# A linear attention and a SiLU MLP on one core: five column blocks in the first load of W1, three in its next, and smaller edits at the start of the kernel

## The chip, the cores and the metric

The kernel runs on one core of a Trainium2 chip. The metric is the time of one execution on the device, in microseconds. The kernel before was run three times; the median is what the changed kernel is compared with. A core has five engines that run their own instruction streams: TensorE (PE, matmuls; PEld is its weight loads), VectorE (DVE), ScalarE (ACT), GpSimd (POOL) and SyncE (SP). They meet at semaphores. Transfers between HBM and the core's SBUF are issued by an engine's queue and run on 16 DMA engines; here SP and ScalarE issue through one kind of queue, GpSimd through another.

## What is computed

The inputs are q, k and v of 8 batches, 8 heads, 576 positions and 64 columns, and two weight matrices, W1 (512 x 2048) and W2 (2048 x 512), all float32. The attention is a linear one: q goes through a softmax over its 64 columns, k through a softmax over the positions, and

```python
kv = np.einsum('bhsd,bhse->bhde', k_s, v)
x = np.einsum('bhsd,bhde->bhse', q_s, kv)     # then heads side by side: 4608 x 512
h = x @ w_in
g = h * (1.0 / (1.0 + np.exp(-h)))
out = g @ w_out                                # 4608 x 512, float32
```

Nearly all the arithmetic is in the two products with W1 and W2.

## The kernel before

The rows of x are worked on in nine chunks (t = 0 to 8) of 512. Chunk 0 is done plainly, with W1 and W2 as they are; its first layer takes all 576 positions of batch 0, so that chunk 1 has only 448 left. The chunks after it use a scheme of seven products per block (`group`, `prod`) that replaces eight by seven and needs sums and differences of blocks of the weights (`ws_op`, `t_op`) and of the data (`xs_op`, `s_op`), which VectorE makes.

The work's order is a list written out by hand, `ORDER`: a string of names, each bound to a small function, called in turn. What one engine does follows that list in its order; across engines only the data's dependences count. So a name that moves in the list past names of other engines keeps its place on its own engine.

The names around the change:

- `lq0.0`, `lk0.0`, `lv0.1.0` and so on load halves of q, k and v of a batch (line 151); those of batch 0 are issued by SP, those of batches 1 and 2 by GpSimd, later ones by SP again.
- `gate` (line 627) is a tiny copy on GpSimd that reads the first half of k of batch 0, so that GpSimd's weight loads start after that has landed.
- `W1a0`, `W1a1`, `W1b`, `W1c`, `W1d` load W1 (line 566). They are issued by GpSimd because they cast from float32 to float16 on the way. W1 has 16 column blocks of 128 columns and 4 row chunks c of 128 rows. Before, W1a0 brings blocks 0 to 3 of chunks 0 and 1, W1a1 the same blocks of chunks 2 and 3, and W1b, W1c and W1d bring four blocks each, all chunks. `W2a` to `W2d` load W2 (line 572) behind them.
- The first layer of chunk 0: `w{fb}.0` and `w{fb}.1` (`wide_mm`, line 306) are the matmuls of column block fb with chunks 0 and 1, then 2 and 3, four each; `h{fb}` (line 319) is the tanh on ScalarE; `v{fb}` (line 322) combines it on VectorE. Each block has a pair of PSUM banks given by `WIDE`; the next block in that pair must wait for the `v` of the one before. `p{fb}` (line 444) is the second layer of chunk 0.
- `vc0.1a`, `vc0.1b`, `vc0.1c` cast the last half of v of batch 0 to bf16 (lines 142 and 144): c takes one pair of heads on GpSimd, a and b share the other pair between ScalarE and VectorE by position blocks j (nine of them). `kv0.1.0` and `kv0.1.1` (line 247) are the matmuls on them; `kc0.1` divides by the sums; `X0.1` (line 281) makes the second half of x of chunk 0; `x0.0a`, `x0.1a` (ScalarE) and `x0.0v`, `x0.1v` (VectorE) copy x out of PSUM.
- In batch 2: `lq2.1` loads the second half of q, `eq2.1` (line 162) is its exp on ScalarE, `z2.1` (lines 206 and 210) its sums and reciprocals on VectorE. In chunk 1, `s1...` (line 142 or 144) copies a pair of PSUM banks to SBUF, `a1...` (line 402) adds another pair to it, and the next `g1...` (line 424) into these banks waits for that. `p15` stands among them in the list.
- `touch` reads a few scattered elements of k, v and W1 at the very start, 64 each, ahead of the large loads; nothing reads what it brings.

Of the kernel before, what the change touches and what calls it, by code (L numbers as in the profile page):

```python
# [16 lines left out]

ORDER = """
    lq0.0 lq0.1 lk0.0 lv0.0 lk0.1 lv0.1.0 lv0.1.1 gate W1a0 W1a1 W1b W1c heat0 eq0.0.0 z0.0.0 eq0.0.1 z0.0.1 eq0.1
    n0.0 ek0.0 z0.1 tr0.0 vc0.0 heat1 n0.1 tc0.0b kv0.0 tc0.0a kc0.0 tr0.1 ek0.1 vc0.1b X0.0 tc0.1b  # L20
    vc0.1a vc0.1c W1d lq1.0 lq1.1 W2a kv0.1.0 kv0.1.1 kc0.1 tc0.1a x0.0v X0.1 x0.0a x0.1v w0.0 w2.0 w1.0 x0.1a W2b1 lk1.0 w1.1 h1 w0.1 w3.0 w2.1
    W2b2 w3.1 h0 v1 v0 w5.0 w5.1 w4.0 w4.1 h2 v2 h3 w6.0 w6.1 h5 v3 h4 v5 w7.0 w7.1 h7 WS1.1 w9.0 v4 h6 w9.1 WS0.1
    w8.0 w8.1 v7 lk1.1 h9 h8 w11.0 v6 eq1.0.0 w11.1 v9 v8 h11 WS1.2 w10.0 lv1.1 w10.1 v11 w12.0 w12.1 eq1.0.1 W2c1
    h10 w13.0 lv1.0 v10 w13.1 w15.0 h12 h13 qp1a w15.1 v12 qp1b h15 v13 w14.0 eq1.1.0 z1.0 w14.1 eq1.1.1 p0 WS0.3 p1
    v15 z1.1.0 WS1.4 W2c2 z1.1.1 h14 lq2.0 n1.0 p2 ek1.1 n1.1 p3 v14 p4 vc1.1b tr1.0 ek1.0 tc1.0a p5 p6 W2d vc1.1a
    p7 p8 gcopy tr1.1 WS1.3 lq2.1 vc1.0 p9 T1 tc1.1a tc1.0b tc1.1b kv1 WS0.2 p10 kc1 xt1.0 xt1.1 lk2.0 eq2.0 x1.1v
    p11 x1.0a g1.1.1 x1.3v x1.2a s1.1.0a xs1.1 xs1.2 g1.1.2 p12 z2.0 eq2.1 g1.1.6 xs1.3 lk2.1 xs1.4 s1.1.1a p13 z2.1
    lv2.0 p14 lv2.1 ek2.0 n2.0 ek2.1 n2.1 vc2.0 a1.1.0 g1.1.7 p15 s1.1.2v tq2 po2v g1.1.5 a1.1.2 g1.1.4 po1a po3v
    lk3.0 vc2.1 po0a m3 u1.1.4 mu3 T3 g1.1.3 m2 lq3.0 u1.1.2 m1 u1.1.0 lq3.1 a1.1.1 m0 mu1 mu0 lk3.1 mu2 lv3.0
    u1.1.1 T2 kv2 kc2 m5 mu5 T4 m4 mu4 m7 X2.0 lv3.1 WS0.4 vc3.1 mu7 X2.1 x2.1a x2.0v m6 x2.2v os0 x2.3a vc3.0 mu6  # L30
    g2.1.1 ek3.0 b1.2.0 b1.1.0 xs2.1 xs2.2 s2.1.0v S1.1 g2.1.6 g2.1.2 S1.2 xs2.3 xs2.4 b1.1.1 eq3.1 b1.2.1 s2.1.1a
    a2.1.0 g2.1.7 ek3.1 g2.1.5 lk4.0 eq3.0 z3.1 g2.0.2 s2.1.2a g2.1.4 sa1 a2.1.2 g2.1.3 n3.1 u2.1.4 b1.6.1 os1 z3.0
    a2.1.1 g2.0.1 u2.1.0 b1.6.0 n3.0 lq4.0 u2.1.2 wa1 s2.0.0a b1.5.0 lk4.1 S1.3 kv3 u2.1.1 S1.4 sb1 g2.0.6 tq3
# [30 lines left out]
    wb7 S8.1b e1.1 o7.0 S8.1a b7.4.1 S8.2a sa8 S8.2b e2.0 wl7v e6.0 S8.3 o7.1 e6.1 e2.1 sb8 e5.0 waE0 S8.4 qa00g
    qa01s e7.0 waE1 e7.1 qa11g qa10a e5.1 sc8 wcE0 e3.0 wcE1 qc01g wxE0 qc11a e3.1 wbE0 qc00a wxE1 qb00g qb01s e4.0
    wbE1 qc10s qb10g e4.1 qb11s wlE0a ql01a ql00s wlE1a ql11a ql10s
"""


# [1 line left out]
def kernel(  # L71
# [9 lines left out]
    nc = tc.nc  # L81
# [4 lines left out]
    J = S // P  # L86
# [45 lines left out]
    T3 = B12  # L132
# [165 lines left out]
        o0 = pieces(t)[0][3]  # L298
        copy(eng, XTS[t % 2][:, c, o0:TCH], PS[:, XBANK[c], o0:TCH])

    WIDE = (4, 2, 0, 6) * 4

    def wide_mm(fb, cs):
        for n in range(2):
            for c in cs:
                nc.tensor.matmul(  # L306
                    out=PS[:, WIDE[fb] + n, 0:S // 2],
                    lhsT=W1[:, c, fb * 128:(fb + 1) * 128],
# [241 lines left out]
    def touch(i, x, eng):  # L550
        rows4 = x.rearrange("(a p z) f -> p a z f", a=4, p=16)
        eng.dma_start(out=touched[:, i, :, None], in_=rows4[:, :, 0, 0:1])
# [144 lines left out]
    for t in range(1, NCH):  # L697
# [6 lines left out]
        for g in range(2):  # L704
            n = f"{t}.{g}."
# [123 lines left out]
```

## Time and profile before

| what | value |
|---|---|
| median of 3 runs | 256.89 us (256.43 to 257.05) |
| the profiled execution's own time | 257.51 us |
| its span, first to last instruction | 255.7 us |
| granted TensorE clock, mean | 0.999 of full speed |
| read from HBM, written to it | 36.70 MB, 9.44 MB |

The time of an execution has 1.8 us that lie outside the span. A row of a timeline gives the start and the length in us, the engine and line, the operation, the tensors written and read with their shape, the number of instructions merged into the row, and in brackets how long the engine was idle before and what ended that. Matmuls overlap each other, so the busy time of a row is longer than the time from its start to the next row's start. A row of DMA issues gives the tensor, the queue, the number, the size of one and the median time from issue to landing. What releases an instruction is inferred from semaphores, so a chain can name a neighbour of the true cause.

### The profile page before, as it was taken

How to read it: one execution, taken by the hardware profiler on the slowest of the kernel's cores; microseconds unless marked ns; L12 is line 12 of the kernel's file. 1: busy time of each engine (PE TensorE's matmuls, PEld its weight loads, DVE VectorE, ACT ScalarE, POOL GpSimd, SP SyncE). 2: the span in 40 equal slices, each digit the busy share in tenths (PEclk: the TensorE clock that was granted, in tenths of full speed). 3: DMA queues.
4: the chain of work that ended last, by engine and by line, in shares of the span. 5: the costliest groups of instructions: out<-in, count | busy, mean ns of one | idle time of the engine just before them, and what ended most of it. 6: DMA issues, size and time to landing. Idle time of an engine off the chain costs nothing.

```text
span 255.7 us, 6428 instructions
## 1 busy us (share of the span) xinstructions
PE 247.9 (97%) x2712; PEld 204.3 (80%) x2712; DVE 205.7 (80%) x277; ACT 190.6 (75%) x226; POOL 66.7 (26%) x64
## 2 busy tenths in 40 slices
PE   7789999999999999999999999999999999999994
PEld 3367755666888888888888888888888888888883
DVE  3868998899999998998987986896569836886752
ACT  4765867899999999999879979737587666664411
POOL 2563872540360631530083040006000000000022
PEclk9999999999999999999999999999999999999999
DMA  7999999879959947996964950021807000700365
GB/s 231 350 200 298 270 337 328 310 150 382 388 117 242 404 158 181 349 307 165 301 246 87 243 198 3 3 61 24 170 6 160 6 0 4 154 11 3 69 139 124
DMA packets 36205, 45.90 MB, mean 180 GB/s; under 512 B 16448, under 2 KB 21248, under 8 KB 36176
## 3 DMA queue, kind: packets, MB, share of 16 engines
q1 hardware_dynamic: 29424, 33.56, 45.1%
q0 software_dynamic: 6192, 11.60, 17.6%
q10 hardware_dynamic: 560, 0.33, 0.6%
q8 instruction: 21, 0.34, 0.6%
q14 instruction: 8, 0.07, 0.1%
HBM read 36.70 MB, written 9.44 MB: 180 GB/s over the span
## 4 chain that ended last, share of the span: by engine, by line
PE 89%; DMA 7%; DVE 1%; POOL 1%; ACT 1%; SPq 0%; issue 0%; ACTq 0%
PE PS L502 37%; PE PS L424 35%; PE PS L444 5%; PE PS L306 5%; DMA W<-in_moe_w_in_dram 4%; DMA kt<-in_k_dram 3%; PE PS L334 2%; PE PS L247 2%; PE PS L281 2%; DMA out_dram<-ow 1%; POOL W L566 1%; DVE h L144 0%; PE PS L233 0%; SPq L151 0%; DVE ow L763 0%; ACT ow L776 0%
## 5 line engine op out<-in xcount | busy, mean ns | idle before, releaser
L402 DVE TENSOR_TENSOR h<-PS,h 128x1024 f32<-128x1024 f32 (+1 forms) x45 | 54.1, 1205 | 9.5 <-PE PS L424 7.8
L502 PEld LDWEIGHTS <-GT 128*128 128x128 f16 x512 | 50.0, 98 | 6.0
L424 PEld LDWEIGHTS <-WS 128*128 128x128 f16 x480 | 46.6, 98 | 6.8 <-issue 1.0
L408 ACT ACTIVATE GT<-h 128x1024 f16<-128x1024 f32 (+1 forms) x45 | 46.7, 1050 | 0.9 <-DVE h L402 0.8
L502 PE MATMUL PS<-W,GT 128*128 128x256 f16 x384 | 47.2, 273 | 0.0
L424 PE MATMUL PS<-XS,WS 128*128 128x256 f16 (+1 forms) x360 | 45.0, 272 | 0.0
L142 ACT COPY h<-PS 128x1024 f32<-128x1024 f32 (+1 forms) x31 | 31.1, 1003 | 16.9 <-PE PS L424 15.8
L502 PEld LDWEIGHTS <-S 128*128 128x128 f16 x384 | 37.1, 98 | 4.7
L424 PEld LDWEIGHTS <-W 128*128 128x128 f16 x360 | 35.1, 98 | 4.5 <-issue 0.2
L215 POOL TENSOR_TENSOR eq<-eq,rzq 128x1152 bf16<-128x1152 bf16 x13 | 27.7, 2139 | 36.0 <-DVE rzq L210 35.8
L144 POOL CAST vaug<-vt 128x1152 bf16<-128x1152 f32 (+1 forms) x13 | 16.3, 1268 | 61.4 <-DMA vt<-in_v_dram 53.3
L502 PE MATMUL PS<-T,S 128*128 128x256 f16 x256 | 32.0, 273 | 0.0
L424 PE MATMUL PS<-XT,W 128*128 128x256 f16 (+1 forms) x240 | 29.9, 272 | 0.0
L144 DVE COPY h<-PS 128x1024 f32<-128x1024 f32 (+1 forms) x14 | 17.0, 1212 | 8.6 <-PE PS L424 3.7
L162 ACT ACTIVATE eq<-qt 128x1152 bf16<-128x1152 f32 (+1 forms) x19 | 18.8, 1008 | 4.6 <-DMA qt<-in_q_dram 4.6
L781 POOL DMA_DIRECT2D out_dram<-ow x5 | 2.7, 545 | 70.0 <-DVE ow L763 70.0
L167 ACT ACTIVATE ek<-kt 128x1152 bf16<-128x1152 f32 x16 | 18.4, 1161 | 3.3 <-DMA kt<-in_k_dram 3.2
L408 ACT ACTIVATE GT<-PS 128x1024 f16<-128x1024 f32 (+1 forms) x15 | 15.2, 1014 | 6.6 <-PE PS L424 6.5
L206 DVE TENSOR_REDUCE zq<-eq 128x18 f32<-128x1152 bf16 x13 | 17.5, 1346 | 1.2 <-ACT eq L162 0.9
L306 PE MATMUL PS<-XT,W 128*128 128x288 f16 x128 | 16.0, 286 | 0.4 <-DMA W<-in_moe_w_in_dram 0.4
L502 PE MATMUL PS<-T,GT 128*128 128x256 f16 x128 | 16.3, 273 | 0.0
L502 PE MATMUL PS<-W,S 128*128 128x256 f16 x128 | 16.1, 273 | 0.0
(86 smaller groups left out, 332.8 us busy)
## 6 DMA issues: line engine op xcount, KB each, us to landing
out_dram<-ow SPq DMA_DIRECT2D x64, 128.0 KB, 3.3
qt<-in_q_dram SPq DMA_DIRECT2D x12, 576.0 KB, 5.7
kt<-in_k_dram SPq DMA_DIRECT2D x12, 576.0 KB, 7.1
vt<-in_v_dram SPq DMA_DIRECT2D x11, 576.0 KB, 6.9
qt<-in_q_dram POOLq DMA_DIRECT2D x4, 576.0 KB, 11.9
kt<-in_k_dram POOLq DMA_DIRECT2D x4, 576.0 KB, 12.6
vt<-in_v_dram POOLq DMA_DIRECT2D x4, 576.0 KB, 12.1
W<-in_moe_w_in_dram POOLq DMA_DIRECT2D x3, 512.0 KB, 10.4
```

The source lines that it names most:

```text
L142: eng.copy(out=o, in_=i)
L144: eng.tensor_copy(o, i)
L162: nc.scalar.activation(out=half(st[b]["eq"], cc)[:, :, g0:g1], in_=jgd(b, "qt", cc)[:, :, g0:g1], func=ACT.Exp)
L167: nc.scalar.activation(out=half(ek, cc), in_=jgd(b, "kt", cc), func=ACT.Exp)
L206: nc.vector.reduce_sum(out=z, in_=e, axis=AX.X)
L215: eng.tensor_tensor(out=e, in0=e, in1=r[:, :, :, None].to_broadcast([128, J, 2, D]), op=ALU.mult)
L306: nc.tensor.matmul(out=PS[:, WIDE[fb] + n, 0:S // 2], lhsT=W1[:, c, fb * 128:(fb + 1) * 128], rhs=XTS[0][:, c, n * (S // 2):(n + 1) * (S / ...
L402: nc.vector.tensor_tensor(out=four(t, i), in0=group_bank(t, g), in1=four(t, i), op=ALU.add)
L408: nc.scalar.activation(out=group_out(t, f, n), in_=x, func=ACT.Silu, scale=1.0 / XS)
L424: nc.tensor.matmul(out=PS[:, bank + p // 2, (p % 2) * HT:(p % 2) * HT + width(t)], lhsT=a[:, c, p * 128:(p + 1) * 128], rhs=bb[:, c, 0:wid ...
L444: nc.tensor.matmul(out=PS[:, 2 + tb, :], lhsT=GTS[t % 2][:, fc, tb * 128:(tb + 1) * 128], rhs=W2[:, fc, :], start=(fc == 0), stop=(fc == N ...
L502: nc.tensor.matmul(out=PS[:, bank, m * HN:(m + 1) * HN], lhsT=a[:, fc, m * 128:(m + 1) * 128], rhs=bb[:, fc, :], start=(first and fc == 0) ...
```

## The change

Five things are edited. The two loads W1a0 and W1a1 bring five column blocks each instead of four, and W1b three instead of four. Blocks 4 and 5 trade places: block 4 now comes ahead of block 5 in the list, with its matmuls, tanh and combination, and their PSUM banks trade places with them. In the list `x0.1a` comes ahead of `x0.1v` and of block 0's matmuls. Of the nine position blocks of v's last cast ScalarE takes four and VectorE five; before it was five and four. The small read of W1 is issued on ScalarE's queue, behind those of k and v, and no longer on GpSimd's.

```diff
-    vc0.1a vc0.1c W1d lq1.0 lq1.1 W2a kv0.1.0 kv0.1.1 kc0.1 tc0.1a x0.0v X0.1 x0.0a x0.1v w0.0 w2.0 w1.0 x0.1a W2b1 lk1.0 w1.1 h1 w0.1 w3.0 w2.1
-    W2b2 w3.1 h0 v1 v0 w5.0 w5.1 w4.0 w4.1 h2 v2 h3 w6.0 w6.1 h5 v3 h4 v5 w7.0 w7.1 h7 WS1.1 w9.0 v4 h6 w9.1 WS0.1
+    W1d lq1.0 lq1.1 W2a kv0.1.0 kv0.1.1 kc0.1 tc0.1a x0.0v X0.1 x0.0a x0.1a x0.1v w0.0 w2.0 w1.0 W2b1 lk1.0 w1.1 h1
+    w0.1 w3.0 w2.1 W2b2 w3.1 h0 v1 v0 w4.0 w4.1 w5.0 w5.1 h2 v2 h3 w6.0 w6.1 h4 v3 h5 v4 w7.0 w7.1 h7 WS1.1 w9.0 v5
...
-    WIDE = (4, 2, 0, 6) * 4
+    WIDE = (4, 2, 0, 6, 2, 4, 0, 6) + (4, 2, 0, 6) * 2
...
-    touch(2, w_in, nc.gpsimd)
+    touch(2, w_in, nc.scalar)
...
-    for x, eng, g, j0, j1 in (("a", nc.scalar, 1, 0, 5), ("b", nc.vector, 1, 5, J), ("c", nc.gpsimd, 0, 0, J)):
+    for x, eng, g, j0, j1 in (("a", nc.scalar, 1, 0, 4), ("b", nc.vector, 1, 4, J), ("c", nc.gpsimd, 0, 0, J)):
...
-    for x, f, n, c0, c1 in (("W1a0", 0, 4, 0, 2), ("W1a1", 0, 4, 2, 4), ("W1b", 4, 4, 0, 4), ("W1c", 8, 4, 0, 4), ("W1d", 12, 4, 0, 4)):
+    for x, f, n, c0, c1 in (("W1a0", 0, 5, 0, 2), ("W1a1", 0, 5, 2, 4), ("W1b", 5, 3, 0, 4), ("W1c", 8, 4, 0, 4), ("W1d", 12, 4, 0, 4)):
```

The rest of the list holds the same names in the same order; its lines are only broken elsewhere.

More of the change, by code (lines that the diff above doesn't have):

```diff
@@ L24 @@
[L24 to L33, printed above, removed]
@@ L64 @@
[L64 to L66 removed]
+    n0.0 ek0.0 z0.1 tr0.0 vc0.0 heat1 n0.1 tc0.0b kv0.0 tc0.0a kc0.0 tr0.1 ek0.1 vc0.1b X0.0 tc0.1b vc0.1a vc0.1c
+    W1d lq1.0 lq1.1 W2a kv0.1.0 kv0.1.1 kc0.1 tc0.1a x0.0v X0.1 x0.0a x0.1a x0.1v w0.0 w2.0 w1.0 W2b1 lk1.0 w1.1 h1
@@ new lines @@
+    w0.1 w3.0 w2.1 W2b2 w3.1 h0 v1 v0 w4.0 w4.1 w5.0 w5.1 h2 v2 h3 w6.0 w6.1 h4 v3 h5 v4 w7.0 w7.1 h7 WS1.1 w9.0 v5
+    h6 w9.1 WS0.1 w8.0 w8.1 v7 lk1.1 h9 h8 w11.0 v6 eq1.0.0 w11.1 v9 v8 h11 WS1.2 w10.0 lv1.1 w10.1 v11 w12.0 w12.1
+    eq1.0.1 W2c1 h10 w13.0 lv1.0 v10 w13.1 w15.0 h12 h13 qp1a w15.1 v12 qp1b h15 v13 w14.0 eq1.1.0 z1.0 w14.1
+    eq1.1.1 p0 WS0.3 p1 v15 z1.1.0 WS1.4 W2c2 z1.1.1 h14 lq2.0 n1.0 p2 ek1.1 n1.1 p3 v14 p4 vc1.1b tr1.0 ek1.0
+    tc1.0a p5 p6 W2d vc1.1a p7 p8 gcopy tr1.1 WS1.3 lq2.1 vc1.0 p9 T1 tc1.1a tc1.0b tc1.1b kv1 WS0.2 p10 kc1 xt1.0
@@ new lines @@
+    xt1.1 lk2.0 eq2.0 x1.1v p11 x1.0a g1.1.1 x1.3v x1.2a s1.1.0a xs1.1 xs1.2 g1.1.2 p12 z2.0 eq2.1 g1.1.6 xs1.3
+    lk2.1 xs1.4 s1.1.1a p13 z2.1 lv2.0 p14 lv2.1 ek2.0 n2.0 ek2.1 n2.1 vc2.0 a1.1.0 g1.1.7 p15 s1.1.2v tq2 po2v
+    g1.1.5 a1.1.2 g1.1.4 po1a po3v lk3.0 vc2.1 po0a m3 u1.1.4 mu3 T3 g1.1.3 m2 lq3.0 u1.1.2 m1 u1.1.0 lq3.1 a1.1.1
+    m0 mu1 mu0 lk3.1 mu2 lv3.0 u1.1.1 T2 kv2 kc2 m5 mu5 T4 m4 mu4 m7 X2.0 lv3.1 WS0.4 vc3.1 mu7 X2.1 x2.1a x2.0v m6
+    x2.2v os0 x2.3a vc3.0 mu6 g2.1.1 ek3.0 b1.2.0 b1.1.0 xs2.1 xs2.2 s2.1.0v S1.1 g2.1.6 g2.1.2 S1.2 xs2.3 xs2.4
@@ new lines @@
+    u4.0.1 xs5.1 g5.1.1 xs5.2 wb3 b3.4.1 s5.1.0v o2.1 ek7.1 g5.1.2 kc6 g5.1.6 wl3a xs5.3 xs5.4 a5.1.0 lv7.0 b4.2.0
+    s5.1.1a lv7.1 b4.1.0 S4.1 eq7.1 g5.1.7 ek7.0 b4.2.1 s5.1.2v o3.1 g5.1.5 S4.2 b4.1.1 u5.1.0 a5.1.2 g5.1.4 sa4
+    g5.0.2 o3.0 u5.1.4 wa4 g5.1.3 S4.3 u5.1.2 vc7.1 g5.0.1 b4.6.0 a5.1.1 vc7.0 s5.0.0a b4.6.1 a5.0.0 u5.1.1 g5.0.6
+    S4.4 b4.5.0 s5.0.1a b4.5.1 sb4 u5.0.0 g5.0.7 g5.0.5 s5.0.2v b4.7.0 eq7.0 a5.0.2 b4.7.1 z7.1 g5.0.4 sc4 g5.0.3
+    b4.4.0 a5.0.1 u5.0.4 b4.4.1 wc4 u5.0.1 X6.0 X6.1 kv7 x6.0v u5.0.2 x6.3v b4.3.0 x6.1a kc7 b4.3.1 x6.2a xs6.1
@@ new lines @@
+    S7.3 g8.1.3 u8.1.4 g8.0.2 a8.1.1 u8.1.2 g8.0.1 u8.1.1 b7.6.0 s8.0.0v b7.6.1 wa7 g8.0.6 a8.0.0 sb7 b7.5.0 s8.0.1a
+    S7.4 b7.7.0 g8.0.7 g8.0.5 s8.0.2v b7.7.1 a8.0.2 b7.5.1 sc7 u8.0.0 g8.0.4 wc7 g8.0.3 u8.0.4 b7.4.0 a8.0.1 u8.0.2
+    b7.3.0 u8.0.1 b7.3.1 e1.0 wb7 S8.1b e1.1 o7.0 S8.1a b7.4.1 S8.2a sa8 S8.2b e2.0 wl7v e6.0 S8.3 o7.1 e6.1 e2.1
+    sb8 e5.0 waE0 S8.4 qa00g qa01s e7.0 waE1 e7.1 qa11g qa10a e5.1 sc8 wcE0 e3.0 wcE1 qc01g wxE0 qc11a e3.1 wbE0
+    qc00a wxE1 qb00g qb01s e4.0 wbE1 qc10s qb10g e4.1 qb11s wlE0a ql01a ql00s wlE1a ql11a ql10s
```

57 lines of the change are left out of this document (25 added, 32 removed).

## The prediction

> **What bounds the kernel now.** I read the head of the page first, then the chain that ended last in order of time, then the timelines of TensorE, ScalarE and VectorE where the chain names something other than TensorE, and last the loads.
>
> ```profile
> span 255.7 us, 6428 instructions
> PE 247.9 (97%) x2712; PEld 204.3 (80%) x2712; DVE 205.7 (80%) x277; ACT 190.6 (75%) x226; POOL 66.7 (26%) x64
> ```
>
> TensorE is busy for 97% of the span, so a gain must start its stream earlier or close a hole in it, and then survive to the end. The chain names one load ahead of the long stretches of matmuls, and the timeline of PE (start, length, line, count, idle time before) shows what it costs:
>
> ```profile
> 10.04 9.22 DMA W<-in_moe_w_in_dram
> ...
> 50.43 1.09 DVE h L144
> ```
>
> ```profile
> 14.81 4.09 PE L306 MATMUL PS<-XT,W 128*128 128x288 f16 x32
> 19.31 11.93 PE L306 MATMUL PS<-XT,W 128*128 128x288 f16 x96 [0.40 <-DMA W<-in_moe_w_in_dram]
> 31.08 4.48 PE L444 MATMUL PS<-W,GT 128*128 128x512 f16 x20
> ```
>
> Line 306 is the first layer of batch 0: sixteen column blocks of eight matmuls. Blocks 0 to 3 run from 14.81; then W1b, issued at 10.04, lands 9.22 later at 19.26, and blocks 5, 4, 6 and so on run without a hole until line 444 starts at 31.08. From start to start that is 11.77 us for 96, or 0.1226 us each. The 32 before would have been done feeding at 14.81 + 32 x 0.1226 = 18.73, so the hole is 0.58 us in starts (0.40 between busy times).
>
> Does a gain there reach the end? The chain's DVE piece at 50.43 made me look at 45 to 52, first PE, then what feeds VectorE (ACT, DVE rows), then the load behind that (POOL's issue, and its time to landing):
>
> ```profile
> 45.43 1.03 PE L444 MATMUL PS<-W,GT 128*128 128x512 f16 x4
> 46.29 0.93 PE L424 MATMUL PS<-XS,WS 128*128 128x224 f16 x8
> 47.06 1.89 PE L444 MATMUL PS<-W,GT 128*128 128x512 f16 x8
> ...
> 49.55 1.03 PE L444 MATMUL PS<-W,GT 128*128 128x512 f16 x4
> 50.57 0.93 PE L424 MATMUL PS<-XS,WS 128*128 128x224 f16 x8
> 51.56 0.93 PE L424 MATMUL PS<-XS,W 128*128 128x224 f16 x8
> ```
>
> ```profile
> 46.72 1.16 ACT L162 ACTIVATE eq<-qt 128x1152 bf16<-128x1152 f32 x1 [0.96 <-DMA qt<-in_q_dram]
> ```
>
> ```profile
> 47.92 1.35 DVE L206 TENSOR_REDUCE zq<-eq 128x18 f32<-128x1152 bf16 x1 [0.89 <-ACT eq L162]
> 49.31 0.27 DVE L210 RECIPROCAL rzq<-zq 128x18 f32<-128x18 f32 x1
> 49.49 1.03 DVE L402 TENSOR_TENSOR h<-PS,h 128x896 f32<-128x896 f32 x1
> 50.43 1.08 DVE L144 COPY h<-PS 128x896 f32<-128x896 f32 x1
> ```
>
> ```profile
> 34.67 0.73 POOL L151 DMA_DIRECT2D qt<-in_q_dram  x1
> ```
>
> ```profile
> qt<-in_q_dram POOLq DMA_DIRECT2D x1, 576.0 KB, 12.0
> ```
>
> Four matmuls of line 444 take 0.86 from start to start (45.43 to 46.29), eight of line 424 take 0.77 (46.29 to 47.06). The p15 of 49.55 is thus fed by 50.41, but the next group starts at 50.57, just after VectorE's addition (a1.1.0) ends at 50.52 and frees its banks: a wait of 0.16. That group is fed by 51.34, yet the following one starts at 51.56, after the copy (s1.1.2v) ends at 51.51: another 0.22. The busy rows overlap and hide both. VectorE is dense from 47.92, where it had idled 0.89 for eq2.1; that had idled 0.96 on ScalarE for the load lq2.1, which lands at 34.67 + 12.0 = 46.7. **So around 51 us the kernel hangs on a load, and TensorE arrives there 0.38 us too early already.** The loads before it are back to back: the share of the DMA engines (next to last column) never falls below one.
>
> ```profile
> core 0: us, PE busy (x) PEld busy (x) DVE busy (x) ACT busy (x) POOL busy (x), PEclk, DMA share, GB/s
> ...
> 12.00:24.00 12.00, 10.74 (x127) 7.93 (x125) 7.99 (x15) 7.29 (x13) 6.47 (x9) 1.00 1.20 231
> 24.00:36.00 12.00, 12.00 (x90) 8.20 (x88) 11.38 (x18) 8.76 (x16) 9.32 (x10) 1.00 1.14 307
> 36.00:47.00 11.00, 11.00 (x147) 6.44 (x144) 9.72 (x19) 8.19 (x12) 3.20 (x5) 1.00 1.11 333
> ```
>
> **The change part by part.**
>
> *Five and three blocks.* The 0.58 us hole sits ahead of the fifth block because that block is in W1b. With five blocks in W1a0 and W1a1, each of them is 320 KB instead of 256, and W1b 384 instead of 512; the megabyte of the three is the same, so I take W1b's landing as it is, 19.26.
>
> ```profile
> 8.55 3.00 POOL L566 DMA_DIRECT2D W<-in_moe_w_in_dram  x4
> ```
>
> ```profile
> W<-in_moe_w_in_dram POOLq DMA_DIRECT2D x1, 256.0 KB, 6.0
> ...
> W<-in_moe_w_in_dram POOLq DMA_DIRECT2D x1, 256.0 KB, 6.5
> ...
> DMA packets 1208, 1.21 MB, mean 202 GB/s; under 512 B 41, under 2 KB 1207, under 8 KB 1207
> ```
>
> The four issues take 0.75 each, so W1a0 (8.55) lands at 14.5 and W1a1 (9.3) at 15.8. Between 13 and 19 us the queue writes 202 GB/s, so 64 KB more take 0.32: W1a0 at 14.84, W1a1 (two times 64 KB behind) at 16.48. Both now come late: the first block could start at 14.76 (next edit) and starts at about 14.89; block 1's second half (w1.1, the thirteenth matmul) could start at 14.89 + 12 x 0.1226 = 16.36 and waits until 16.53. From there 116 matmuls without a hole end their feeding at 16.53 + 14.22 = 30.75, against 31.08: **0.33 us gained at the start of line 444**, not 0.58. Block 5 is due at 16.53 + 28 x 0.1226 = 19.96, with 0.7 to spare to W1b. The issues on POOL that wait for these landings go out up to 0.65 later, into a queue that lands things 12 us after their issue: no cost while the backlog stands.
>
> By the fit of the Trainium skill (page "DMA: Bandwidth & Descriptors", section "Anatomy of one DMA — SWDGE (gpsimd) path": 2.0 us plus bytes over 436 GB/s), 64 KB more would be an estimated 0.15, W1a1 would land at 16.13 and delay nothing, and the gain would be 0.63; the trace's 202 GB/s for these casting loads disagrees with that rate.
>
> *Blocks 4 and 5 swapped* in the list and in their banks, and x0.1a moved up: the banks come round in the order they had, ScalarE's own order is unchanged but for the two swapped tanh. Cost 0.
>
> *VectorE's five ninths of the last v cast.*
>
> ```profile
> 12.86 0.47 ACT L142 CAST vaug<-vt 128x320 bf16<-128x320 f32 x1 [0.15 <-DMA vt<-in_v_dram]
> 12.86 0.29 DVE L144 CAST vaug<-vt 128x256 bf16<-128x256 f32 x1 [0.71 <-DMA vt<-in_v_dram]
> ...
> 37.61 0.67 ACT L142 CAST vaug<-vt 128x576 bf16<-128x576 f32 x1
> ...
> 37.42 0.75 DVE L144 CAST vaug<-vt 128x576 bf16<-128x576 f32 x1
> ```
>
> By the 576-column rows, 64 columns are 0.05 on ScalarE and up to 0.12 on VectorE. ScalarE's part ends at 13.28 instead of 13.33, VectorE's at 13.24 to 13.27 instead of 13.15: the later of both gains 0.05, which the matmuls of line 247, X0.1 and block 0 inherit (14.81 to 14.76). VectorE's qT copy behind it slips by the same 0.1, and only X0.1, just ahead of 14.81, needs it. W1a0's landing then eats the gain.
>
> *The small read of W1 on ScalarE's queue.*
>
> ```profile
> kvn<-in_k_dram ACTq DMA_DIRECT2D x1, 0.2 KB, 3.2
> kvn<-in_moe_w_in_dram POOLq DMA_DIRECT2D x1, 0.2 KB, 5.0
> kvn<-in_v_dram ACTq DMA_DIRECT2D x1, 0.2 KB, 4.2
> ...
> out_dram<-ow POOLq DMA_DIRECT2D x5, 64.0 KB, 2.1
> ...
> vt<-in_v_dram SPq DMA_DIRECT2D x2, 288.0 KB, 8.4
> ```
>
> ```profile
> 1.33 0.67 POOL L552 DMA_DIRECT2D kvn<-in_moe_w_in_dram  x1 [0.89 <-POOLq L813]
> 1.34 0.43 ACTq L552 DMA_DIRECT2D kvn<-in_v_dram  x1
> ...
> 3.56 1.35 SPq L151 DMA_DIRECT2D vt<-in_v_dram  x2
> ```
>
> (The last column of the first five rows is us to landing.) POOL loses an issue of 0.67; the next issue there that anything waits for is W1a0's at 8.55. ScalarE's queue gets a third issue of some 0.43 ahead of the first exp, which waits for q anyway. It is one more on the two hardware queues: SP's last two issues took 1.35 for two because the second waited for an earlier load's landing; now the one before it may wait as well, up to 1 us. Both land 8.4 us after their issue, behind loads that keep the engines full: 0. The open price is whether POOL's first real load, W1a0, then pays for being the first of its queue. Below: 0, as all loads run on the same engines. Above: the small read took 5.0 on POOL, against 4.2 for v's on ScalarE (1.33 and 1.34, at the same time) and 2.1 for POOL's stores at the end, so between 0.8 and 2.9. I take 0, since the 4.2 shows that most of the 5.0 is the crowd of that moment. The Trainium skill says the same on that page, section "Issuing engines are not separate DMA queues": the issuing engine saves only issue time.
>
> **The sum.** Start of line 444: -0.33. At 50.57 and 51.56: TensorE, already 0.38 early, becomes 0.7 early; lq2.1 lands when it did, since the bytes ahead of it are the same. After 51.56 nothing moves. Span 255.7, change 0 (with -0.05 for small things). The profiled execution took 257.51, 0.62 over the median of 256.89; against the median I predict **256.8**.
>
> **The rivals.** 0.3% is 0.77 us, about what a measurement of this kernel can tell from no change.
>
> *A, likeliest, no change:* as summed, 256.5 to 257.2. For it: the idle times before eq2.1 and z2.1. Against: the profiled execution is slower than the median, perhaps just in its loads.
>
> *B, faster:* lq2.1 does not decide, because the loads run sooner (W1's first megabyte is 5.2 us of the queue, now in rows of 2560 and 1536 bytes instead of 2048; 10% on it would be 0.5). TensorE's gain then passes, 0.33, or 0.63 if W1a1 is in time, plus up to 0.38 of the waits at 50 us: 256.6 down to 255.9. It is over 0.3% where the load is at least 0.77 sooner and W1a1 is in time.
>
> *C, slower:* POOL's queue wakes up on W1a0. With s for the delay, W1a1 lands at 16.48 + s, line 444 starts s - 0.33 later, and 0.38 of that is absorbed: s - 0.7. If the DMA engines idle meanwhile, lq2.1 is late by up to s. At s = 0.8 that is 0.1 to 0.8, at 1.5 it is 0.8 to 1.5 (257.7 to 258.4), at 2.9 it is 259.1 and more. It decides from s between 0.8 and 1.5. Against it: the 4.2 of v's read.
>
> **How the numbers follow.** A 0.40; B 0.31, of which 0.23 beyond 0.3%, since row lengths that no row shows may move the queue; C 0.29, of which 0.27 beyond. Faster 0.23, same 0.50, slower 0.27. The range reaches to B's end and into C's middle: 255.9 to 258.1, A's own 256.5 to 257.2.
>
> **What the profile after would show.** Right: no hole at the fifth block; line 444 starting 0.2 to 0.4 sooner; a short wait for W1 at block 0 or at w1.1; the waits before line 424 at 50 us grown to 0.6 or 0.7 with eq2.1 starting at 46.7 as before. Wrong: eq2.1 starting over 0.7 sooner or later, W1a0 landing after 15.6, or a new hole on PE after 52 us.

## The result, and the profile after

The kernel became slower: 257.74 us (median of 12 runs, 257.33 to 258.82) against 256.49 (12 runs, 256.25 to 257.73) for the kernel before on the same chip. The ratio is 1.0046 (1.0029 to 1.0064), or 1.18 us (by the two medians 1.25). The forecast was no change at 256.8, so it missed; the range of 255.9 to 258.1 holds the time.

The head of the page after looks better, if anything:

```profile
span 255.5 us, 6428 instructions
...
PE 247.2 (97%) x2712; PEld 204.7 (80%) x2712; DVE 205.8 (81%) x277; ACT 190.6 (75%) x226; POOL 65.5 (26%) x63
```

TensorE's busy time is 0.7 us less and the span 0.2 us less than before. The two pages are not to be subtracted, though: the profiled execution of before took 257.51, 1.02 above the median of its 12 runs, and that of after 257.33, 0.41 below its own. What the change did must be read place by place.

**The start.** The timeline of PE after (start, length, engine, line, operation, tensors, count) answers to the three rows of line 306 and line 444 before:

```profile
14.71 15.85 PE L306 MATMUL PS<-XT,W 128*128 128x288 f16 x128
30.40 4.48 PE L444 MATMUL PS<-W,GT 128*128 128x512 f16 x20
```

One row of 128 matmuls, no hole: 14.71 + 128 x 0.1226 = 30.40, to the hundredth. Line 444 starts 0.68 sooner than it did. The loads, in the view of the DMA issues after (last column: us from issue to landing), landed at 14.44 (W1a0), 16.04 (W1a1) and 18.45 (W1b):

```profile
W<-in_moe_w_in_dram POOLq DMA_DIRECT2D x2, 320.0 KB, 6.3
...
W<-in_moe_w_in_dram POOLq DMA_DIRECT2D x1, 384.0 KB, 8.4
```

The last casts of v, with five position blocks on VectorE, in the timelines of ACT and DVE after; line 306 starts 1.92 behind the landing of that load (12.79), where it was 1.98:

```profile
12.81 0.41 ACT L142 CAST vaug<-vt 128x256 bf16<-128x256 f32 x1 [0.17 <-DMA vt<-in_v_dram]
12.81 0.49 DVE L144 CAST vaug<-vt 128x320 bf16<-128x320 f32 x1 [0.72 <-DMA vt<-in_v_dram]
```

**Around 50 us.** The timelines of PE, ACT and DVE after, at the place where the kernel before hung on a load of q:

```profile
48.87 1.03 PE L444 MATMUL PS<-W,GT 128*128 128x512 f16 x4
49.73 0.93 PE L424 MATMUL PS<-XS,WS 128*128 128x224 f16 x8
50.50 0.93 PE L424 MATMUL PS<-XS,W 128*128 128x224 f16 x8
```

```profile
44.98 1.17 ACT L162 ACTIVATE eq<-qt 128x1152 bf16<-128x1152 f32 x1
```

```profile
46.27 1.35 DVE L206 TENSOR_REDUCE zq<-eq 128x18 f32<-128x1152 bf16 x1
```

The load lq2.1 landed at 44.83 instead of 46.7, ScalarE's exp starts at once (no idle time in brackets), VectorE's sum 1.65 us sooner, and the two waits of before are gone: from 48.87 the starts are 0.86 and 0.77 apart, which is the work itself. The second group that read 51.56 before reads 50.50 here, 1.06 sooner. That lead is still there at the end of the last matmul: 250.92 against 252.02, 1.10 sooner.

**The end.** And there it is lost. From the last matmul's end to the end of the span it took 3.69 us before and 4.60 after. Two pieces of that grew. The first is the time from the last matmul to the last landing of a store, 2.76 before and 3.25 after. The DMA view of the last stretch (DMA queues with packets, MB and share, then issues with KB and us to landing), before and after; before's fetch on q14 shows only in a later window, from 254 on:

```profile
out_dram<-ow SPq DMA_DIRECT2D x4, 64.0 KB, 2.2
out_dram<-ow ACTq DMA_DIRECT2D x2, 64.0 KB, 2.0
...
q14 instruction: 1, 0.01, 1.4%
```

```profile
q14 instruction: 1, 0.01, 1.6%
...
out_dram<-ow SPq DMA_DIRECT2D x2, 64.0 KB, 2.8
out_dram<-ow ACTq DMA_DIRECT2D x1, 64.0 KB, 2.6
```

There is one fetch of instructions (a packet of 8 KB) near the end of both executions. Before, it starts at 254.35, 2.33 behind the last matmul, when all stores but the last two have landed. After, it starts at 252.31, 1.39 behind the last matmul, in the midst of the last three stores, and takes 755 ns. Those three took 2.96, 2.57 and 2.66 us to land; before it was 2.07, 1.98 and 2.17.

The landings themselves tie the two together. The trace has sixteen updates of its semaphore for every store, as many as there are DMA engines. After, fifteen of them came by 252.94, 253.43 and 253.69 for the last three stores, and the sixteenth at 253.82, 254.00 and 254.17, so 0.88, 0.57 and 0.48 later; before, the sixteenth came 0.02 to 0.03 behind the fifteenth. One share in sixteen of each store is held up. That it is the share of the DMA engine that carried the fetch is inferred: the last packets of the stores run one at a time and are through 0.55 behind the fetch's end.

The second piece is the time from the last landing to the end, 0.93 before and 1.35 after. SP's waits in the last 6 us (us in total, times, the longest), before and after:

```profile
SPq L824 <- DMA out_dram<-ow: 1.0, 3, 0.4
```

```profile
SPq L824 <- DMA out_dram<-ow: 2.0, 1, 2.0
```

Before, SP waits for the last stores one after the other, three times. After, it waits once, 2.0 us, for the very last one, and does all its other checks behind that. The times at which SP's checks passed, from the trace (S101 is semaphore 101; the first row is the check ahead of the last store's issue):

```
before                          after
S118 252.57  (not yet the end)  S101 251.46  (not yet the end)
S108 253.27                     S101 254.18  last landing 254.17
S112 253.34                     S104 254.25
S113 253.40                     S105 254.31
S114 253.50                     S106 254.37
S115 253.69                     S107 254.43
S116 254.06                     S108 254.49
S117 254.53                     S109 254.55
S118 254.80  last landing 254.78  S110 254.61
```

The transfers of the two hardware queues, SP's and ScalarE's, share eight semaphores and take them in turn (before, each of S108 and S112 to S118 has 15 of them; after, S101 has 16 and the seven others 15). At the end SP looks at the eight in the order of that round. The kernel before has 120 such transfers, 15 full rounds, so the last store holds the eighth semaphore and SP looks at it last. The kernel after has 121, since the small read of W1 moved over from GpSimd's queue. So the last store holds the first semaphore, SP stands at it for 2.0 us, and seven more checks of 0.06 us follow: 7 x 0.06 = 0.42.

0.49 and 0.42 make 0.91 of the 1.18. The moved read itself, at the start, did what was forecast:

```profile
1.80 0.45 ACTq L552 DMA_DIRECT2D kvn<-in_moe_w_in_dram  x1
```

### The profile page after: what moved, and what is told of

Its sections match the earlier page's. It is cut to its first block, busy times and chain, and to the rows that moved or that the text cites. A ratio compares the mean times of both kernels' runs of the same rounds, so it can differ in the third digit from the quotient of the medians.

```text
span 255.5 us, 6428 instructions
## 1 busy us (share of the span) xinstructions
PE 247.2 (97%) x2712; PEld 204.7 (80%) x2712; DVE 205.8 (81%) x277; ACT 190.6 (75%) x226; POOL 65.5 (26%) x63
## 4 chain that ended last, share of the span: by engine, by line
PE 91%; DMA 5%; ACT 1%; DVE 0%; POOL 0%; ACTq 0%; issue 0%
PE PS L502 37%; PE PS L424 36%; PE PS L306 6%; PE PS L444 5%; DMA vt<-in_v_dram 3%; PE PS L334 2%; PE PS L247 2%; PE PS L281 2%; DMA qt<-in_q_dram 1%; DMA out_dram<-ow 1%; PE PS L233 0%; DVE ow L763 0%; ACT ow L776 0%; POOL vaug L144 0%; ACT sc L748 0%; ACTq L781 0%
## 5 line engine op out<-in xcount | busy, mean ns | idle before, releaser
L424 PEld LDWEIGHTS <-WS 128*128 128x128 f16 x480 | 46.7, 98 | 6.5 <-issue 0.6
L408 ACT ACTIVATE GT<-h 128x1024 f16<-128x1024 f32 (+1 forms) x45 | 46.7, 1049 | 0.9 <-DVE h L402 0.7
L144 POOL CAST vaug<-vt 128x1152 bf16<-128x1152 f32 (+1 forms) x13 | 15.6, 1215 | 62.5 <-DMA vt<-in_v_dram 31.6
```

Source lines behind the costliest of these rows:

```text
L144: eng.tensor_copy(o, i)
L408: nc.scalar.activation(out=group_out(t, f, n), in_=x, func=ACT.Silu, scale=1.0 / XS)
L424: nc.tensor.matmul(out=PS[:, bank + p // 2, (p % 2) * HT:(p % 2) * HT + width(t)], lhsT=a[:, c, p * 128:(p + 1) * 128], rhs=bb[:, c, 0:wid ...
```

## The experiments

Theory at the outset: the small read of W1 on ScalarE's queue costs the time, at the end and not at the start. Its rivals: the column blocks and the swap cost it (the read is innocent); and, of the two pieces of the end, the one or the other is an accident of one execution. In the table, "L444" is the start of line 444, "store" the time from the last matmul to the last landing, "rest" from the last landing to the end, "fetch" the start of the last instruction fetch behind the last matmul; all from one profile each. HW is the number of transfers on the two hardware queues, ACT the number of ScalarE's instructions against before.

| kernel | HW | ACT | L444 | last matmul ends | store | rest | fetch | ratio to before (95%) |
|---|---|---|---|---|---|---|---|---|
| before | 120 | 0 | 31.08 | 252.02 | 2.76 | 0.93 | 2.33 | |
| after | 121 | +1 | 30.40 | 250.92 | 3.25 | 1.35 | 1.39 | 1.0046 (1.0029 to 1.0064) |
| after_again | 121 | +1 | 30.21 | 251.10 | 3.34 | 1.34 | 1.40 | 1.0047 (1.0033 to 1.0061) |
| e1_touch_only | 121 | +1 | 29.91 | 250.99 | 3.27 | 1.35 | 1.36 | 1.0051 (1.0037 to 1.0065) |
| e2_all_but_touch | 120 | 0 | 29.74 | 250.85 | 2.77 | 0.92 | 2.30 | 1.0005 (0.9995 to 1.0015) |
| e3_store_gpsimd | 120 | +1 | 29.72 | 251.31 | 3.10 | 0.92 | 1.37 | 1.0017 (1.0008 to 1.0026) |
| e4_no_v_read | 120 | 0 | 29.67 | 250.85 | 2.77 | 0.91 | 2.30 | 0.9994 (0.9986 to 1.0003) |
| e4_again | 120 | 0 | 30.51 | 250.91 | 2.76 | 0.91 | 2.34 | 1.0010 (0.9992 to 1.0027) |
| e5_one_more_exp | 120 | +1 | 31.16 | 251.66 | 2.97 | 0.92 | 1.39 | 1.0060 (1.0032 to 1.0087) |
| e6_store_sp | 121 | 0 | 30.27 | 251.60 | 2.75 | 1.36 | 2.30 | 1.0021 (1.0011 to 1.0032) |
| e7_store_off_act | 120 | -1 | 30.66 | 251.99 | 2.77 | 0.91 | 2.50 | 1.0018 (1.0005 to 1.0031) |
| e7_again | 120 | -1 | 30.55 | 251.10 | 2.78 | 0.91 | 2.49 | 1.0008 (0.9994 to 1.0022) |
| e8_exp_behind_reads | 120 | +1 | 30.29 | 251.64 | 2.89 | 0.93 | 1.38 | 1.0028 (1.0007 to 1.0050) |
| e9_k_before_w2 | 120 | 0 | 30.16 | 251.13 | 2.75 | 0.90 | 2.33 | 1.0012 (0.9996 to 1.0029) |

**The read alone, and all but the read.** First, the kernel before with nothing but the small read moved:

```diff
-    touch(2, w_in, nc.gpsimd)
+    touch(2, w_in, nc.scalar)
```

> The kernel before, with the small read of W1 alone moved to ScalarE's queue. Two theories of the 1.2 us lost. Tail: this read is a third transfer on the hardware queues, so every later one of them takes the next semaphore of the round, the last store gets the first of the list that SP checks at the end, and all other checks come behind its landing (in the changed kernel 1.35 us from the last landing to the end of the span, against 0.93 before); besides, ScalarE has one instruction more, and an 8 KB instruction fetch falls among the last stores. Start: the loss is in the first 50 us, by W1's other cut or by the POOL queue waking up on W1a0. Tail expects +0.4 to +1.0 us against the kernel before, with TensorE's last matmul where it was, and 1.3 us from the last landing to the end. Start by the cut of W1 expects 0 (within 0.3 us); start by a late queue expects W1a0 to land after 15.3.

It measured 257.51 against 256.27, 1.0051: the whole loss. Its last matmul ended at 250.99, not where it did in the profile of before (252.02); that is taken up under "Why the rest gains nothing". Second, the kernel after with only that line put back:

```diff
-    touch(2, w_in, nc.scalar)
+    touch(2, w_in, nc.gpsimd)
```

> The changed kernel with the small read of W1 back on POOL's queue, all else of the change kept. Tail expects the loss gone: -0.3 to +0.2 us against the kernel before, and 0.9 us from the last landing to the end of the span. Start by the cut of W1 expects +0.8 to +1.3 still; start by a late queue expects W1a0 to land about where it did, and the time of the kernel before.

256.36 against 256.27, 1.0005: no difference. So the loss belongs to the read, and the rest of the change is worth nothing that can be measured. The DMA view of the last stretch and SP's waits of e1:

```profile
q14 instruction: 1, 0.01, 1.7%
...
out_dram<-ow ACTq DMA_DIRECT2D x2, 64.0 KB, 2.3
out_dram<-ow SPq DMA_DIRECT2D x2, 64.0 KB, 2.8
```

```profile
SPq L824 <- DMA out_dram<-ow: 2.0, 1, 2.0
```

and of e2, where the fetch comes in the window behind that of the issues:

```profile
out_dram<-ow ACTq DMA_DIRECT2D x2, 64.0 KB, 2.0
out_dram<-ow SPq DMA_DIRECT2D x2, 64.0 KB, 2.1
...
q14 instruction: 1, 0.01, 1.5%
```

```profile
SPq L824 <- DMA out_dram<-ow: 1.1, 4, 0.5
```

Both pieces come with the read and go with it.

**The round alone.** Two runs separate the pieces. e3 is the kernel after with one store of the output moved from SP's queue to GpSimd's, so that 120 hardware transfers are left while ScalarE keeps its extra instruction; e6 is the kernel before with one store moved the other way, which makes 121 and leaves ScalarE alone:

```diff
-    ... S8.4 qa00g qa01s e7.0 ...
+    ... S8.4 qa00g qa01g e7.0 ...
```

> The changed kernel, with one of the first stores of the last tile (qa01) issued by POOL and not by SP. That takes one transfer off the hardware queues behind the third small read, so the round of semaphores stands at its end as it did before, while the start is the changed kernel's to the instruction. Tail expects 0.9 us from the last landing to the end of the span (1.35 in the changed kernel) and 0.4 less than the changed kernel, +0.5 to +0.9 against the kernel before; if the fetch among the last stores is gone as well, 0 to +0.3. Start in either form expects no change against the changed kernel: +1.0 to +1.4.

```diff
-    ... sb8 e5.0 waE0 S8.4 qa00g
+    ... sb8 e5.0 waE0 S8.4 qa00s
```

> The kernel before, with the first store of the last tile (qa00) issued by SP and not by POOL: one more transfer on the hardware queues, ScalarE's instructions as before. The round of semaphores theory expects ten checks behind the last landing and 1.35 us from it to the end (0.93 before), with the last landing still 2.77 behind the last matmul: +0.35 to +0.5 us. If the fetch moves with the round, +0.9 and 3.2. If neither matters, within 0.2 us of the kernel before.

e3: the rest is 0.92 again, but the fetch stays at 1.37 and the store at 3.10, and the ratio is 1.0017, +0.44 us (0.21 to 0.67): part of the loss, a little less than the +0.5 to +0.9 expected. e6: the rest is 1.36, the fetch (2.30) and the store (2.75) are as before, and the ratio is 1.0021, +0.54 us (0.28 to 0.82). So the turned round alone costs about 0.5, of which the trace shows 0.43 in its checks. SP's waits of e6 have the form of after's, one wait and nothing more:

```profile
SPq L824 <- DMA out_dram<-ow: 1.5, 1, 1.5
```

**The extra instruction alone.** The other piece should need no DMA at all, only one instruction more on ScalarE. The kernel before got a second dummy exp, first ahead of the small reads (e5), then behind them (e8). It changes nothing that is computed.

```diff
     nc.scalar.activation(out=dummy, in_=dummy, func=ACT.Exp)
+    nc.scalar.activation(out=dummy, in_=dummy, func=ACT.Exp)
```

> The kernel before, with the one-element exp at the start of ScalarE issued twice: one more ScalarE instruction of 0.2 us in an idle stretch, no more transfers. It takes the fetch apart from the round of semaphores. If the 8 KB fetch near the end is ScalarE's and comes earlier by its instruction count, it stands 1.4 us behind TensorE's last matmul (2.3 in the kernel before), the last store lands 3.1 to 3.3 us behind that matmul (2.76 before), and the last landing to the end stays 0.92: +0.3 to +0.6 us. If the fetch goes with the number of transfers or the order of SP's checks, nothing changes: 2.77, 0.92 and within 0.2 us of the kernel before.

```diff
     touch(2, w_in, nc.gpsimd)
+    nc.scalar.activation(out=dummy, in_=dummy, func=ACT.Exp)
```

> The kernel before with the one-element exp issued once more, now behind the small reads, so that ScalarE has one instruction more and the small reads start when they did (issued ahead of them it delayed them by 1.4 us and all loads of q, k and v by 0.5, so that run showed two things at once). If ScalarE's count alone brings the 8 KB fetch forward: the fetch 1.4 us behind the last matmul, the last landing 3.0 to 3.3 behind it instead of 2.77, 0.92 from there to the end, +0.2 to +0.6 us. If the count is not the cause: 2.77, 0.92 and within 0.2 us of the kernel before.

In both the fetch moved (1.39 and 1.38 behind the last matmul), as in after, with the rest at 0.92 and 0.93. e5's ratio of 1.0060 (+1.54 us) is more than the +0.3 to +0.6 expected of this piece, and its timeline of ACT shows a second thing: the extra exp held back the small reads behind it.

```profile
2.26 0.20 ACT L547 ACTIVATE dummy<-dummy 1x1 f32<-1x1 f32 x1
2.27 0.40 ACTq L553 DMA_DIRECT2D kvn<-in_k_dram  x1
2.71 0.44 ACTq L553 DMA_DIRECT2D kvn<-in_v_dram  x1
```

They are issued 1.37 later than before (0.90 and 1.34), and q's first load landed at 5.02 instead of 4.55. So e5 mixes two things; what the late reads cost by themselves was not measured. e8 does not mix them: the reads go out as before, and it measured 1.0028 (medians 257.05 and 256.55, +0.50). Its last stores, by the DMA view:

```profile
q14 instruction: 1, 0.01, 1.2%
...
out_dram<-ow ACTq DMA_DIRECT2D x2, 64.0 KB, 2.1
out_dram<-ow SPq DMA_DIRECT2D x2, 64.0 KB, 2.5
```

The last three took 2.61, 2.21 and 2.31 us, longer than before's 2.07, 1.98 and 2.17. In this trace that makes the store only 0.13 longer (2.89, where 3.0 to 3.3 was expected), less than in e3 (0.34), whose fetch starts at the same place, or in after (0.49).

The traces show what this size goes with, the fetch's own duration. The sixteenth update of the last store came behind the fifteenth by:

| | e8 | e5 | e3 | after | e1 | after_again | the eight others |
|---|---|---|---|---|---|---|---|
| the fetch took, us | 0.56 | 0.61 | 0.67 | 0.76 | 0.80 | 0.82 | 0.37 to 0.61 |
| sixteenth behind fifteenth, us | 0.13 | 0.20 | 0.31 | 0.48 | 0.52 | 0.57 | 0.01 to 0.06 |
| store longer than before, us | 0.13 | 0.21 | 0.34 | 0.49 | 0.51 | 0.58 | -0.01 to 0.02 |

In the eight others the fetch starts 2.3 to 2.5 behind the last matmul, when the stores' data are through or lack at most 0.12 us. In the six the data are through only 0.54 to 0.55 behind the fetch's end. So the extra instruction costs something by itself, by way of the fetch: 0.13 to 0.58 by the traces, 0.18 to 1.28 by e8's interval. Why the fetch takes 0.56 in one and 0.82 in another is not known. By the medians e6 and e8 add up to 0.55 + 0.50 = 1.05 of 1.25, by the ratios to 0.54 + 0.72 = 1.26 of 1.18.

Why the fetch moves by 0.94 (2.33 to 1.39) can be read from ScalarE's own rows at the end of before:

```profile
251.60 0.47 ACTq L781 DMA_DIRECT2D out_dram<-ow  x1
...
252.53 0.49 ACTq L781 DMA_DIRECT2D out_dram<-ow  x1
```

ScalarE's last two stores are issued 0.93 apart. The fetch follows the later of them by 1.82 before; after, it follows the earlier one, issued at 250.50, by 1.81. A fetch that comes at a certain count of ScalarE's instructions would be reached one store sooner in this way when there is one instruction more ahead of it.

**Both pieces undone by other means.** If the account is right, the kernel after must also be mended without touching the read of W1: by taking one of ScalarE's stores to GpSimd's queue (e7), or by leaving out the small read of v (e4), which nothing reads. Each takes away one hardware transfer. From ScalarE e4 takes one instruction, which makes as many as before, and e7 two by its trace, the store and the wait ahead of it, one fewer than before and than its expectation says.

```diff
-    ... e7.1 qa11g qa10a e5.1 ...
+    ... e7.1 qa11g qa10g e5.1 ...
```

> The changed kernel whole, with one store of the last tile (qa10) issued by POOL and not by ScalarE: ScalarE's instructions and the transfers on the hardware queues are both as many as before, while the three small reads stay where the change puts them. If the round and ScalarE's count are the whole loss: 2.77 from the last matmul to the last landing, 0.92 from there to the end, and -0.2 to +0.2 us against the kernel before. If the third small read costs by itself, or the cut of W1 does: +0.4 to +1.2.

```diff
-    touch(1, v[0].rearrange("h s d -> (h s) d"), nc.scalar)
```

> The changed kernel without the small read of v: two transfers on the hardware queues as before, ScalarE's instructions as many as before, and POOL's queue still begins with W1a0. Tail expects -0.3 to +0.3 us against the kernel before. Start, in either form, expects +0.8 to +1.4, as W1's cut and POOL's queue are those of the changed kernel; so would a theory that v's first load needs its small read.

e4: 0.9994 (0.9986 to 1.0003), all of the loss gone, fetch at 2.30 and rest 0.91. e7: fetch at 2.50 and rest 0.91, so both pieces are gone, but 1.0018 (1.0005 to 1.0031), +0.46 us. The last matmul of that profile ended 1.1 later than in e4's, so something ahead of the end was slower. To see whether this belongs to the kernel, e7 and e4 ran once more side by side; the changed kernel had run once more beside the first e7:

> The changed kernel with store qa10 on POOL once more, beside the changed kernel without v's small read on the same chip. Its tail was mended and yet it came out 0.46 us over the kernel before. If the third small read costs by itself at the start: again +0.3 to +0.7, and as much over the kernel without v's read. If the 0.46 was the spread of the start (k's first load landed at 7.6 in the first four runs and at 8.1 to 8.4 in the others, whatever the kernel): -0.2 to +0.2.

> The changed kernel without v's small read once more, on this chip. Tail alone expects what it gave, -0.3 to +0.2 us against the kernel before; if W1's cut gains by itself, below -0.2 with an interval that excludes none.

> The changed kernel as it is, beside the others on one chip. Tail expects its 3.25 and 1.35 us at the end again and +0.9 to +1.3 us against the kernel before; if the slow last landings of its first profile were chance, 2.77 and 1.35 and +0.4.

e7_again measured 1.0008 (0.9994 to 1.0022), e4_again 1.0010 (0.9992 to 1.0027): no difference for either. The first e7's 0.46 did not repeat; its first k of batch 1 (lk1.0) had landed 0.59 later than e7_again's (32.68 and 32.09). The changed kernel did repeat: 1.0047.

**Why the rest gains nothing.** e1 and e2 ran on one chip; e1 has the blocks of before and the moved read, e2 the new blocks and the read where it was. In e1 line 444 started at 29.91 and in e2 at 29.74 (29.72 in e3, which has the new blocks and the moved read): the hole was worth 0.17 to 0.19 there. Then timelines of PE and ACT of e2:

```profile
40.20 0.80 PE L247 MATMUL PS<-vaug,ek 64*64 64x65 bf16 x72 [0.45 <-ACT vaug L142]
...
51.34 0.92 PE L334 MATMUL PS<-XT,W 128*128 128x448 f16 x4
```

```profile
34.77 2.22 ACT L167 ACTIVATE ek<-kt 128x1152 bf16<-128x1152 f32 x2 [3.48 <-DMA kt<-in_k_dram]
```

and of PE of e1:

```profile
39.79 0.80 PE L247 MATMUL PS<-vaug,ek 64*64 64x65 bf16 x72
...
51.21 0.92 PE L334 MATMUL PS<-XT,W 128*128 128x448 f16 x4
```

At 40 us e2 waits 0.45 for ScalarE, which had waited 3.48 for a load of k (lk1.1), and at line 334's first matmul it is 0.13 behind e1. So in that profile a load decides here too, but it is k's at 40 us. The last run asked whether that load could be had sooner: e4 with W2b2 and lk1.1 traded in the list.

```diff
-    w0.1 w3.0 w2.1 W2b2 w3.1 ...   ... v7 lk1.1 h9 ...
+    w0.1 w3.0 w2.1 lk1.1 w3.1 ...   ... v7 W2b2 h9 ...
```

> The changed kernel without v's small read, and in the list W2b2 and lk1.1 trade places, so that k of batch 1 is fetched ahead of a part of W2 that the second layer needs only at 35 us. In the mended kernels TensorE waits 0.35 to 0.45 us at 40 us for v's last cast, which waits on ScalarE behind the exp of that load. If that wait is what eats the gain of W1's cut, the load lands some 1.3 us sooner, the wait is gone, and the time is 0.2 to 0.5 us below that of the same kernel without the swap. If the next load (lq2.1, 50 us) takes its place: less than 0.1.

Timelines of ACT and PE of e9, and of PE of e4_again, which ran beside it:

```profile
33.54 2.22 ACT L167 ACTIVATE ek<-kt 128x1152 bf16<-128x1152 f32 x2 [1.82 <-DMA kt<-in_k_dram]
...
45.45 1.16 ACT L162 ACTIVATE eq<-qt 128x1152 bf16<-128x1152 f32 x1 [0.19 <-DMA qt<-in_q_dram]
```

```profile
40.03 1.08 PE L247 MATMUL PS<-vaug,ek 64*64 64x65 bf16 x72
...
51.45 0.92 PE L334 MATMUL PS<-XT,W 128*128 128x448 f16 x4
```

```profile
40.24 0.81 PE L247 MATMUL PS<-vaug,ek 64*64 64x65 bf16 x72
...
51.38 0.92 PE L334 MATMUL PS<-XT,W 128*128 128x448 f16 x4
```

ScalarE has k 0.82 sooner and TensorE's group at 40 us starts 0.21 sooner, yet line 334 starts at 51.45 against 51.38, and e9 measured 1.0012 (0.9996 to 1.0029): no difference. The lead is lost inside that group: in its middle it waits until 40.33 for VectorE's copy of qT, which ended at 40.28 in e9 and at 39.89 in e4_again, and the row of line 444 behind it starts at 41.05 against 40.98. So k's load was not the only thing that TensorE would have had to wait for there.

All 14 profiles say the same. From line 334's first matmul to the last matmul it is 199.5 to 199.9 us in 13 of them (200.5 in e8), so the front has had its whole effect by 51 us. And where a profile stands at 51 us goes with the landing of the load lk1.0, not with the start of line 444:

| profiles | lk1.0 lands | line 444 starts | line 334 starts |
|---|---|---|---|
| new blocks: after, after_again, e2, e3, e4, e4_again, e7_again, e9 | 31.72 to 32.18 | 29.67 to 30.55 | 50.96 to 51.61 |
| old blocks: e1, e8 | 31.70, 32.08 | 29.91, 30.29 | 51.21, 51.15 |
| new blocks: e7 | 32.68 | 30.66 | 52.26 |
| old blocks: before, e5, e6 | 32.72 to 32.79 | 30.27 to 31.16 | 52.00 to 52.33 |

With line 444 at 30.27 to 30.66, line 334 starts at 51.15 to 51.47 where k came early and at 52.00 to 52.26 where it came late, with either layout of W1. The loads behind lk1.0 on its queue move with it: lq2.1, the load of the prediction, landed at 44.83 to 45.52 in the first ten profiles and at 45.99 to 46.70 in the last four. So the table shows that the loads go with the place at 51 us, and not which of them decides it. No version among these was measurably faster than the kernel before.

## Why the prediction was wrong

**The step that failed** is the one on the small read: "Both land 8.4 us after their issue, behind loads that keep the engines full: 0", with the open price put on W1a0's landing alone, and with it the sum's "After 51.56 nothing moves". It followed the moved read to the transfers around it, at the start, and there it was right that it costs nothing. It did not ask what one transfer and one instruction more do to everything that is counted afterwards. In the profile after they measured +0.42 (the round of eight semaphores, SP's checks behind the last landing) and +0.49 (ScalarE's last fetch of instructions among the last stores), 250 us later; e6 and e8 show each alone, e1 both. That the range nevertheless holds 257.74 is luck: its upper part was there for rival C. The trace before held half of a warning: 120 transfers on the two queues, and SP waiting three times at the end with the last landing in its last wait.

The rule of the Trainium skill that the prediction set beside this step (page "DMA: Bandwidth & Descriptors", section "Issuing engines are not separate DMA queues": the issuing engine saves only issue time) agrees with the landing times of the loads here: the first halves of q and k landed at 4.48 and 8.30 after, and at 4.55 and 8.38 before. Taken as the whole price of the move it gives 0, and e1 gives 1.31 (1.0051 x 256.27 less 256.27).

Step by step:

- *The hole of line 306 closes*: right, one row of 128. *W1a1 late at 16.48, gain of 0.33*: too pessimistic for the profile after. There it landed at 16.04; w1.1 was due at 14.71 + 12 x 0.1226 = 16.18, so nothing waited, and the start gained 0.68. In other profiles with the new blocks both waits are as forecast: in e4_again, e7, e7_again and e9 block 0 starts 0.05 behind W1a0's landing, and in these and in after_again a hole of 0.07 to 0.10 stands at the thirteenth matmul. The price of 64 KB at 202 GB/s held between the two landings, which are 1.60 apart instead of 1.31. It did not hold for W1a0, which was put at 14.84 and landed at 14.44; on the chip of e1 to e4 it landed at 13.64 with four blocks (e1) and at 13.71 to 13.87 with five (e2, e3, e4), so 0.07 to 0.23 later. The Trainium skill's fit (page "DMA: Bandwidth & Descriptors", section "Anatomy of one DMA — SWDGE (gpsimd) path"; an estimated 0.15 for 64 KB) lies within that, and not near the 0.29 between the two landings.
- *VectorE's five ninths, 0.05 gained*: right. Line 306 starts 1.98 behind the landing of v's last load with the old split (before, e1, e5, e6, e8) and 1.92 to 1.94 with the new one where W1a0 is in time (after, after_again, e2, e3, e4).
- *W1b's landing as it is*: 18.45 instead of 19.26 here, and 18.09 to 18.77 in 11 of the 14 profiles, with either layout. With the old layout the hole ahead of line 444 was 0.58 in before and 0 to 0.17 in e1, e5, e6 and e8 (start of line 444 less start of line 306 less 15.69). So the gain that the change was to have was mostly a property of one execution, 1.02 above its median, and the prediction knew only 0.62 of that.
- *The load lq2.1 lands when it did, 46.7, and eats the gain at 50 us*: wrong in place, right in kind. It landed at 44.83, and the waits were gone instead of grown to 0.6 or 0.7. Eq2.1 started 1.74 sooner, which the prediction had named as a sign that it would be wrong. Yet what the start gains is not to be found at 51 us in the runs either, where the loads go with the place; and "no change" for the blocks, the swap and the cast is what e2 measured (1.0005).
- *Rival B, faster*: its condition held in the profile (lq2.1 1.9 sooner, W1a1 in time) and the last matmul ended 1.10 sooner than in the profile before. But with the old blocks e1's ended as early (250.99), and e2's median gained nothing.
- *Rival C, slower because GpSimd's queue wakes up on W1a0*: wrong. W1a0 landed at 14.44, before its matmul was due. C had the right side and the right edit, by a mechanism that did not occur.

What stays open: 0.91 of the 1.18 us is seen in the two tails, and the rest lies within the interval (0.74 to 1.64). That the fetch is ScalarE's is read from its time, which follows ScalarE's instruction count in all 14 profiles (+1: 1.36 to 1.40 behind the last matmul; 0: 2.30 to 2.34; -1: 2.49 and 2.50) and not SP's or GpSimd's; that it slows the stores is read from their sixteenth updates, late in the six profiles with +1 and in no other. The size of that piece goes with the fetch's duration (0.13 to 0.58 in the traces); why that differs is not known. Nor is it known why the loads of k and q land early or late, which moves the place at 51 us by up to 1.4.

## What to carry to other kernels

A transfer moved from one queue to another is priced at three places: where it runs, in the order in which the end is checked, and in the number of instructions on its new engine. Look at the last microseconds first when a change with no visible cost at its own place makes a kernel slower: compare last matmul to last landing, and last landing to end, and count the transfers on the hardware queues. And before a wait of 0.4 us in one profile is made the base of a sum, ask how far that execution stood from the median; here the hole at 19 us was 0.58 in that one and at most 0.17 in four others of the same layout.

## What the runs showed that was not expected

- The transfers of both hardware queues share eight semaphores in turn, and SP checks them at the end in that order, 0.06 us each. With the last store on the last of the round 0.90 to 0.93 us remain behind its landing, on the first 1.34 to 1.36.
- One 8 KB fetch of instructions takes 0.37 to 0.61 us when it comes 2.3 to 2.5 behind the last matmul and 0.56 to 0.82 among the last stores, and a store in its company takes up to 3.05 us to land instead of 2.07. One of the sixteen updates of that store comes up to 0.99 behind the other fifteen.
- Small reads that go out 1.37 us late (e5) come with q's first load 0.47 later, although nothing waits for what they read.
